# Sliding-window attention and an MLP-mixer on one core: side work planned into two thirds of the MLP, stores of the last batches on GpSimd's queue, more transpositions by DMA, loads begun sooner

## The chip, the core and the metric

The kernel runs on one core of a Trainium2 chip. The core has TensorE (matmuls, into PSUM), VectorE and ScalarE (which empty PSUM and do the elementwise work), GpSimd (here it issues the DMAs that cast), SyncE (SP, here it issues transposing DMAs and stores) and 16 DMA engines that all queues share. The metric is the device time of one execution in microseconds; the median of three runs before the change is 296.96 us.

## The reference

Eight batches of 576 positions and 8 heads of 64. First causal attention over a window of 128 positions with an ALiBi bias per head; then an MLP-mixer on the result (512 channels): a token MLP across positions, a residual, a channel MLP (512 to 1536 to 512), a residual. Inputs and output are float32.

```python
scores = np.matmul(q, k.T) / 8 - slope[h] * |i - j|     # only 0 <= i - j < 128
x = softmax(scores) @ v                                 # then heads side by side: [8, 576, 512]
h = np.maximum(x.T @ w_tok1, 0) @ w_tok2                # 576 -> 256 -> 576
u = x + h.T
out = u + np.maximum(u @ w_ch1, 0) @ w_ch2              # 512 -> 1536 -> 512
```

## The kernel before, in words

Two batches form a pair: 9 blocks of 128 positions, four per batch and one (`TAIL`) that holds the last 64 positions of both. A window of 128 means that a block attends to itself and to the block before it.

For each block `load` brings q, k and v with GpSimd's DMAs, which cast to bf16. `transposes` turns q and k so that the head dimension lies on partitions: on TensorE (8 transpositions, L455, into a PSUM bank that VectorE or ScalarE copies out, L460) or, from the block with number `FROM_QK` = 12 on, by a transposing DMA on SP's queue (L447). `scores` does the score matmuls (L485) into two double banks, ScalarE's exponential (L494) and VectorE's multiplication by the mask table (L500), which holds bias and window. `values` multiplies by v, whose extra column of ones gives the sums (L525), and VectorE divides (L529, L533; ScalarE can, L542).

`token_mix` does the token MLP of a batch (L561 and L568, relu L574 or L575; L599 and L595) and adds x, giving u (L617; for batch 0 with an identity matmul, L602, and a copy, L614). Then u is turned: by TensorE (4 transpositions per block, L634, copies L640) for batches under `FROM_U` = 4, by SP's transposing DMA (L625) for the rest.

`side(b)` is attention and token mixing of batch b. `main(b)` is its channel MLP: 12 hidden tiles of four 512-column matmuls (L682), relu (L687 or L688), three extra tiles for the tail block in odd batches (L697), then for each block 12 matmuls of the second layer in four groups of three (L718), the sum with u (L725), and a store by SP (L734, L732).

Nothing of this order is written by hand. `Plan` records every operation with an engine, a cost in ns, a rank and its buffers, and `Plan.run` lays them out in time: at each step it takes, over all engines, the operation that can start first, and at equal times the one with the lower rank. Buffers are rings; PSUM has four single banks and two double ones (`s0`, `s1`), one for each set of heads. Ranks of `main(b)` and of `side(b + 1)` both run along the length of `main(b)`, the side's over `SPREAD` = 0.93 of it, so the two are interleaved. Loads go out in a fixed order (`LOADS` for the first pair and the weights, then block by block), at most 8 in flight and 10 blocks ahead. An operation with `other` may go to a second engine. `emit` writes the instructions in planned order, and puts matmuls on zeros (L767) into planned gaps of TensorE in the first 60 us. The waits between engines follow from the buffers.

At the start raw q and k of block 0 come as float32 by SP and ScalarE (L347) and VectorE casts them (L396); GpSimd makes the identity and the distance table with five operations (L348 to L353) before its first load, and ScalarE makes the masks from the distances (L357).

Of the kernel before, what the change touches and what calls it, by code (L numbers as in the profile page):

```python
# [10 lines left out]
ALU = mybir.AluOpType  # L11
# [5 lines left out]
SPREAD = 0.93  # L17


class Buf:  # L20
    def __init__(self, ring):
        self.ring, self.slot = ring, None
        self.writers, self.parts, self.users = [], {}, []

    def __call__(self):
        return self.ring.slots[self.slot]


class Ring:
    def __init__(self, slots):  # L30
        self.slots = slots
        self.owner = [None] * len(slots)
        self.log = [[] for _ in slots]

# [8 lines left out]
    def best(self):  # L43
        got = [(t, i) for t, i in ((self.free(i), i) for i in range(len(self.slots))) if t is not None]
        return min(got) if got else None
# [6 lines left out]
class Plan:  # L52
# [3 lines left out]
    def ring(self, name, slots):  # L56
        self.rings[name] = Ring(slots)

    def buf(self, name):
        return Buf(self.rings[name])  # L60
# [45 lines left out]
    def dma(self, emit, descs, packets, makes=(), rewrites=(), order=None):  # L106
        o = self.op("POOL", 550 + 0.33 * descs, emit, 0, makes=makes, rewrites=rewrites,
                    order=order or self.slot())
        o.packets = packets
        return o  # L110

    def run(self):
# [21 lines left out]
        free = {"PE": 1500.0, "ACT": 5600.0, "DVE": 1600.0, "POOL": 2300.0, "SP": 1300.0}  # L134
        server, lanes, sent = SERVER, [], 0
        self.gaps = []
        mode = 0
        todo = len(ops)
        while todo:
            best = None  # L140
            for e, c in cand.items():
                pick = None
                for o in c:
                    if e == "POOL" and o is not pool[sent]:
                        continue
                    t = max(ready[o], free[e])
                    if o.other:
                        mine, its = (o.cost, o.other[1]) if e == o.eng else (o.other[1], o.cost)
                        that = o.other[0] if e == o.eng else o.eng
                        if max(ready[o], free[that]) + its < t + mine - (0 if e == o.eng else 1):  # L150
                            continue
                    for b in o.bufs:
                        if b.slot is None:
                            got = b.ring.best()
                            if got is None:
                                t = None
                                break
                            t = max(t, got[0])
                    if t is None:
                        continue  # L160
                    if e == "POOL" and len(lanes) >= 8:
                        t = max(t, lanes[-8])
                    key = (t if t > free[e] + 1e-6 else free[e], o.rank, o.n)
                    if pick is None or key < pick[0]:
                        pick = (key, o)
                if pick and (best is None or pick[0][0] < best[0][0]):
                    best = pick + (e,)
# [8 lines left out]
            for b in o.bufs:  # L176
                if b.slot is None:
                    b.slot = b.ring.best()[1]
                    b.ring.owner[b.slot] = b
                    b.ring.log[b.slot].append(b)  # L180
            if e == "PE":
                slow = 2.0 if t < WARM else 1.0
                if t > free[e] + 1.0:
                    self.gaps.append((free[e], t))
                    t += 60.0
                elif o.mode != mode:
                    t += 95.0
                mode = o.mode
                o.t0 = t
                free[e] = t + o.cost * slow  # L190
                o.done = free[e] + 165.0
            elif e == "ACT":
                o.t0, free[e], o.done = t, t + o.cost - 115, t + o.cost
            elif e == "DVE":
                o.t0, free[e], o.done = t, t + max(o.cost - 80, 50), t + o.cost
            elif e == "SP":
                o.t0, free[e] = t, t + o.cost
                if o.bus:
                    start = t + 300
                    o.done = start + min(3.3 * o.bus, o.bus + max(server - start, 0)) + 650  # L200
                    server = max(server, start) + o.bus
                else:
                    o.done = t + 2500
            else:
                o.t0 = t
                free[e] = t + o.cost
                server = max(server, t + 1000) + o.packets * PACKET
                o.done = server + 1500
                lanes.append(o.done)
                sent += 1  # L210
# [11 lines left out]
    def emit(self, spin):  # L222
        banks = self.rings["bank"]
# [15 lines left out]
WARM = 9000.0  # L239
HOLD = 2  # L240
FROM_QK = 12
FROM_U = 4
AHEAD = 10
FILL = 60000.0
SERVER = 4700.0
# [8 lines left out]
def kernel(  # L254
# [43 lines left out]
    plan.ring("bank", [psum.tile([P, DM], F32, name=f"bank{i}") for i in range(4)])  # L298
    for e in range(2):
        plan.ring(f"s{e}", [psum.tile([P, 2 * DM], F32, name=f"wide{e}")])  # L300
# [5 lines left out]
    ring("v", AHEAD, [P, H, D + 1])  # L306
# [15 lines left out]
    ident = const.tile([P, P], BF16, name="ident")  # L322
    dist = const.tile([P, 2, P], F32, name="dist")
# [21 lines left out]
    dve_.memset(zero[:, :], 0.0)  # L345
    for raw, t, eng in ((raws[0], q, nc.sync), (raws[1], k, nc.scalar)):
        eng.dma_start(out=raw[:, :, :], in_=rows(t, 0, 0, P))  # L347
    make_identity(nc, ident)  # L348
    nc.gpsimd.iota(dist[:, :, :], pattern=[[-P, 2], [1, P]], base=P, channel_multiplier=-1,
                   allow_small_or_imprecise_dtypes=True)  # L350
    nc.gpsimd.affine_select(out=dist[:, 0, :], in_=dist[:, 0, :], compare_op=ALU.is_gt,
                            fill=1.0e9, base=0, pattern=[[-1, P]], channel_multiplier=1)
    nc.gpsimd.affine_select(out=dist[:, 1, :], in_=dist[:, 1, :], compare_op=ALU.is_ge,  # L353
                            fill=1.0e9, base=0, pattern=[[1, P]], channel_multiplier=-1)
    for e in range(2):
        for i, h in enumerate(HEADS[e]):
            act_.activation(out=masks[e][:, i, :, :], in_=dist[:, :, :], func=ACT.Exp,  # L357
                            scale=-float(slopes[h]))
    for t in plan.rings["v"].slots:
        dve_.memset(t[:, :, D : D + 1], 1.0)  # L360

# [80 lines left out]
    def transposes(pr, blk, rank):  # L442
# [7 lines left out]
        tp = plan.buf("bank")  # L450

        def go():
            for i, n in enumerate("qk"):
                for hp in range(NHP):
                    pe_.transpose(tp().bitcast(BF16)[:, (i * NHP + hp) * P : (i * NHP + hp + 1) * P],  # L455
                                  got()[:, i, 2 * hp : 2 * hp + 2, :].rearrange("p h d -> p (h d)"),
                                  ident[:, :])

        def copy(eng=dve_.tensor_copy):
            eng(out=t().rearrange("p a b -> p (a b)"), in_=tp().bitcast(BF16))  # L460

        plan.op("PE", 8 * 56, go, rank, makes=tp, uses=[got])
        plan.op("DVE", 690, copy, rank, makes=t, uses=[tp], other=("ACT", 1025, lambda: copy(act_.copy)))

    def scores(pr, blk, half, rank, behind=()):
# [3 lines left out]
        sp = [plan.buf(f"s{e}") for e in range(2)]  # L469
# [36 lines left out]
    def values(pr, blk, half, e, pb, rank):  # L506
# [4 lines left out]
        ot, rt = plan.buf("bank"), plan.buf("rt")  # L511
# [10 lines left out]
        def go():  # L522
            mms = [(a, z, kind, vb, i, h) for a, z, kind, vb in work for i, h in enumerate(HEADS[e])]
            for m, (a, z, kind, vb, i, h) in enumerate(mms):
                pe_.matmul(view()[a:z, i, :], lhsT=pb[e]()[:, i, kind, a:z], rhs=vb()[:, h, :],  # L525
# [21 lines left out]
    def token_mix(b, rank):  # L547
# [4 lines left out]
        xt = plan.buf("xt")  # L552
        r1 = plan.buf(f"r1{half}")
        t1 = [plan.buf("bank") for _ in range(NJ)]
        tk = half if (pr == 0) else None
        plan.op("DVE", 260, lambda: dve_.tensor_copy(out=xt()[far, :], in_=xb()[own, TAIL, :]), rank(0),
                makes=xt, reads=[(xb, (TAIL, tk))])
# [8 lines left out]
        def tails():  # L566
            for j, rs, rhs in ((0, own, xb()[own, TAIL, :]), (1, far, xt()[far, :])):
                pe_.matmul(t1[j]()[:, :], lhsT=W1[rs, NC, j * P : (j + 1) * P], rhs=rhs, start=False, stop=True)  # L568

        plan.op("PE", 225, tails, rank(216), adds=t1, reads=[(xb, (TAIL, tk))], uses=[xt], needs=lw1,  # L570
                mode=1)
# [11 lines left out]
        for blk in blocks:  # L583
            wide = b == 0
            if wide and blk < 2:
                hts.append(plan.buf(f"s{blk}"))
            ht = hts[blk % 2] if wide else plan.buf("bank")
# [32 lines left out]
        for blk in blocks:  # L620
# [9 lines left out]
            ut = plan.buf("bank")  # L630
# [40 lines left out]
    def main(b, rank):  # L671
# [4 lines left out]
        r2t = plan.buf("r2t") if half else None  # L676
        for t in range(NHT):
            ct = plan.buf("bank")
# [6 lines left out]
            rk = rank(864)  # L685
            plan.op("PE", 862, go, rk, makes=ct, reads=[(uT, x) for x in blocks if x != TAIL], needs=[lc1[t]])
# [3 lines left out]
            if half and t % 4 == 3:  # L690
                cx = plan.buf("bank")
# [15 lines left out]
        for blk in blocks:  # L707
# [3 lines left out]
            for cols in cuts:  # L711
                o2 = plan.buf("bank")
# [16 lines left out]
                def store(blk=blk, ob=ob, cols=cols):  # L729
                    if blk == TAIL:  # L730
                        for i in range(2):
                            nc.sync.dma_start(out=out[2 * pr + i, NC * P : S, :], in_=ob()[i * R : (i + 1) * R, :])  # L732
                    else:
                        nc.sync.dma_start(out=out[b, (blk % NC) * P : (blk % NC + 1) * P, cols], in_=ob()[:, cols])  # L734

                plan.op("SP", 550, store, rk, uses=[ob])
# [64 lines left out]
```

## Time and profile before

| | |
|---|---|
| runs | 296.24, 296.96, 297.02 us |
| the profiled execution | 296.92 us, span 295.1 us |
| granted TensorE clock | 1.000 |
| TensorE busy | 285.9 us, 2490 matmuls |
| VectorE, ScalarE, GpSimd busy | 159.8, 136.1, 110.1 us |
| hidden layer, L682 | 384 matmuls, 92.9 us |
| second layer, L718 | 396 matmuls of 512 columns, 96.4 us |
| transpositions on TensorE | qk (L455) 104, u (L634) 72 |
| fillers, L767 | 28 |
| transposing DMAs on SP | 24 of qk, 18 of u |
| DMA | 36.67 MB, engines full until about 195 us |

A row of the lines' view gives line, engine, operation, tiles and shapes, the number, then busy us and mean ns of one. A matmul's duration there is longer than the interval from one to the next, since matmuls overlap; intervals are read from the chain of waits, which lists pieces in order of time. "US to landing" is the time from a DMA's issue to its completion.

### The profile page before, as it was taken

Reading aid. Unit: us, or ns where it says so; the run is one execution under the profiler, and the core shown is the slowest. Engines: PE = TensorE matmul, PEld = TensorE weight load, DVE = VectorE, ACT = ScalarE, POOL = GpSimd, SP = SyncE. Lnnn points to the kernel's source line nnn. Section 1 sums busy time; section 2 is a strip of 40 time slices with the busy share of each in tenths; the row PEclk is TensorE's granted clock in tenths of the full one; section 3 lists DMA queues with packets and bytes.
Section 4 is the critical chain, followed back from the end, with each engine's and each line's share of the span. In section 5 each row is a group of like instructions: output and inputs, shape, how many; then the busy total and the mean of one; then the engine's idle time right before and its main releaser. Section 6 shows DMA issues by size and latency. Waiting matters only on the chain.

```text
span 295.1 us, 6147 instructions
## 1 busy us (share of the span) xinstructions
PE 285.9 (97%) x2490; PEld 150.2 (51%) x2490; DVE 159.8 (54%) x364; ACT 136.1 (46%) x236; POOL 110.1 (37%) x140
## 2 busy tenths in 40 slices
PE   7999999999999999999999999999999999999995
PEld 2665454446664555455664445445664445435543
DVE  4697656735674466455773548254873556250022
ACT  5483884218940197008840087107850087105600
POOL 8998495976656257510585008000000000000000
PEclk9999999999999999999999999999999999999999
DMA  9999999999999999999999959955001510042013
GB/s 121 142 148 179 176 161 181 157 189 185 157 137 140 216 169 150 127 195 169 126 117 162 223 106 106 130 109 126 2 2 71 142 38 2 36 122 76 0 71 107
DMA packets 158011, 36.67 MB, mean 124 GB/s; under 512 B 148768, under 2 KB 153504, under 8 KB 157984
## 3 DMA queue, kind: packets, MB, share of 16 engines
q0 software_dynamic: 115376, 17.67, 87.9%
q1 hardware_dynamic: 41568, 18.36, 33.0%
q8 instruction: 19, 0.31, 0.4%
q10 hardware_dynamic: 1040, 0.26, 0.4%
q14 instruction: 8, 0.07, 0.1%
HBM read 35.85 MB, written 9.44 MB: 153 GB/s over the span
## 4 chain that ended last, share of the span: by engine, by line
PE 89%; DVE 5%; ACT 2%; DMA 2%; issue 1%
PE bank L718 31%; PE bank L682 28%; PE wide L485 6%; PE bank L525 5%; PE bank L599 4%; PE bank L561 4%; PE bank L697 4%; PE bank L455 2%; DVE pe L500 2%; DMA raw<-in_q_dram 1%; PE bank L634 1%; ACT pe L494 1%; PE bank L767 1%; PE bank L568 1%; DMA uT<-ub 1%; ACT xb L542 1%
## 5 line engine op out<-in xcount | busy, mean ns | idle before, releaser
L718 PE MATMUL bank<-WC,r 128*128 128x512 bf16 (+1 forms) x396 | 96.4, 373 | 0.0
L682 PE MATMUL bank<-uT,WC 128*128 128x512 bf16 x384 | 92.9, 379 | 2.4 <-DVE xb L533 1.0
L494 ACT ACTIVATE pe<-wide 128x1024 bf16<-128x1024 f32 (+1 forms) x74 | 63.3, 911 | 35.5 <-PE wide L485 35.4
L687 ACT ACTIVATE r<-bank 128x512 bf16<-128x512 f32 x75 | 44.5, 600 | 39.2 <-PE bank L682 36.4
L718 PEld LDWEIGHTS <-r 128*128 128x128 bf16 x396 | 37.2, 98 | 42.2 <-issue 3.1
L725 DVE TENSOR_TENSOR ob<-bank,ub 128x512 f32<-128x512 f32 (+1 forms) x37 | 25.1, 677 | 59.6 <-PE bank L718 59.3
L682 PEld LDWEIGHTS <-WC 128*128 128x128 bf16 x384 | 34.1, 98 | 37.5 <-issue 3.6
L381 POOL DMA_DIRECT2D v<-in_v_dram x40 | 34.5, 867 | 47.9 <-PE bank L525 36.2
L500 DVE TENSOR_TENSOR pe<-pe,mask 128x1024 bf16<-128x1024 bf16 (+1 forms) x66 | 39.3, 612 | 6.8 <-ACT pe L494 6.3
L381 POOL DMA_DIRECT2D qk<-in_q_dram x39 | 33.8, 867 | 15.4 <-DMA qk<-in_k_dram 9.5
L381 POOL DMA_DIRECT2D qk<-in_k_dram x39 | 33.4, 859 | 8.8 <-DMA v<-in_v_dram 3.4
L617 DVE TENSOR_TENSOR ub<-bank,xb 128x512 bf16<-128x512 f32 x32 | 21.7, 688 | 13.4 <-PE bank L599 11.9
L525 PEld LDWEIGHTS <-pe 128*128 128x128 bf16 (+1 forms) x552 | 22.9, 100 | 11.9 <-DVE pe L500 2.3
L525 PE MATMUL bank<-v,pe 128*128 128x65 bf16 (+1 forms) x552 | 26.9, 196 | 0.7 <-DVE xb L533 0.3
L533 DVE TENSOR_TENSOR xb<-bank,rt 128x256 bf16<-128x256 f32 (+1 forms) x62 | 25.6, 422 | 1.3
L688 DVE TENSOR_SCALAR r<-bank 128x512 bf16<-128x512 f32 x21 | 14.5, 688 | 17.6 <-PE bank L682 15.0
L574 ACT ACTIVATE r<-bank 128x512 bf16<-128x512 f32 x8 | 4.8, 597 | 38.8 <-PE bank L568 38.8
L561 PE MATMUL bank<-xb,W 128*128 128x512 bf16 x64 | 21.4, 380 | 0.1
L485 PEld LDWEIGHTS <-qkT 64*128 64x128 bf16 x552 | 15.1, 96 | 12.4 <-issue 8.0
L485 PE MATMUL wide<-qkT 64*128 64x128 bf16 (+1 forms) x296 | 19.8, 222 | 0.7 <-DVE qkT L460 0.7
L529 DVE RECIPROCAL rt<-bank 128x4 f32<-128x4 f32 (+1 forms) x74 | 11.7, 173 | 9.8 <-PE bank L525 9.5
L599 PE MATMUL bank<-r,W 128*128 128x512 bf16 x56 | 16.2, 379 | 0.0
(55 smaller groups left out, 193.6 us busy)
## 6 DMA issues: line engine op xcount, KB each, us to landing
out_dram<-ob SPq DMA_DIRECT2D x31, 256.0 KB, 3.1
v<-in_v_dram POOLq DMA_DIRECT2D x32, 128.0 KB, 7.9
qk<-in_q_dram POOLq DMA_DIRECT2D x31, 128.0 KB, 9.5
qk<-in_k_dram POOLq DMA_DIRECT2D x31, 128.0 KB, 9.4
WC<-in_moe_w_ch_dram POOLq DMA_DIRECT2D x8, 384.0 KB, 8.6
out_dram<-ob SPq DMA_DIRECT2D x10, 128.0 KB, 2.3
qk<-in_q_dram POOLq DMA_DIRECT2D x8, 64.0 KB, 7.3
qk<-in_k_dram POOLq DMA_DIRECT2D x8, 64.0 KB, 7.8
```

Source lines behind the costliest of these rows:

```text
L381: nc.gpsimd.dma_start(out=to()[p0 : p0 + n, :, :], in_=rows(src, b, s0, n))
L485: pe_.matmul(wide(e)[:, i, kind, a:z], lhsT=ts[kb]()[e * D : (e + 1) * D, NHP + i, :], rhs=ts[blk]()[e * D : (e + 1) * D, i, a:z], start=T ...
L494: act_.activation(out=pb[e]()[:, :, lo:, c0:c1_], in_=wide(e)[:, :, lo:, c0:c1_], func=ACT.Exp, scale=scale)
L500: dve_.tensor_tensor(out=o, in0=o, in1=mk[:, :, lo:, c0:c1_], op=ALU.mult)
L525: pe_.matmul(view()[a:z, i, :], lhsT=pb[e]()[:, i, kind, a:z], rhs=vb()[:, h, :], start=m == 0, stop=m == len(mms) - 1, skip_group_check=True)
L533: dve_.tensor_tensor(out=x4[r0:r1_, :, e, :], in0=view()[r0:r1_, :, 0:D], in1=rt()[r0:r1_, :, :].broadcast_to([r1_ - r0, 4, D]), op=ALU.mult)
L561: pe_.matmul(t1[j]()[:, :], lhsT=W1[:, c, j * P : (j + 1) * P], rhs=xb()[:, blk, :], start=c == 0, stop=False)
L599: pe_.matmul(ht()[:, hs], lhsT=W2[:, j, c * P : (c + 1) * P], rhs=r1()[:, j, :], start=j == 0, stop=j == NJ - 1 and not fold)
L682: pe_.matmul(ct()[:, :], lhsT=WC1[:, cb, t * P : (t + 1) * P], rhs=uT()[:, cb, :], start=cb == 0, stop=cb == NCB - 1)
L687: plan.op("ACT", 600, lambda t=t, ct=ct: act_.activation(out=r2()[:, t, :], in_=ct()[:, :], func=ACT.Relu), rk, part=(r2, t), uses=[ct], o ...
L718: pe_.matmul(o2()[:, cols], lhsT=l, rhs=WC2[:, t, cols], start=t == 0, stop=t == NHT - 1)
L725: plan.op("DVE", 160 + 530 * n / DM, lambda blk=blk, o2=o2, ob=ob, cols=cols: dve_.tensor_tensor(out=ob()[:, cols], in0=o2()[:, cols], in1 ...
```

## The change

Ten things are changed together:

- `SPREAD` goes from 0.93 to 0.65: ranks of the next batch's side work run over the first two thirds of the main part.
- `FROM_QK` 12 to 9, `FROM_U` 4 to 2: all qk blocks of the second pair, and u of batches 2 and 3, are turned by SP's DMAs.
- From batch `FROM_P` = 5 on stores go out on GpSimd's queue, behind all loads, except the last two blocks of the last batch.
- GpSimd does only one iota before its loads; VectorE makes distances and identity.
- Block 0 of the first pair is turned in two halves, q and then k, each copied by itself.
- The first three hidden tiles of batch 0 are done in quarter-width pieces, block by block as u is turned.
- Batch 0's token mixing no longer copies the tail rows to the other half; its two tail matmuls run one after the other.
- The planner lets an operation of batch 0's side work go ahead of one that could start sooner (`FIRST`, `GRACE`).
- PSUM is one tile of 8 banks; scores take either of two pairs; v is stored with rows of 128 elements per head instead of 65.
- Planner constants (starting times, SP's cost beside a transposition, `SERVER`).

```diff
-SPREAD = 0.93
+SPREAD = 0.65
...
-        free = {"PE": 1500.0, "ACT": 5600.0, "DVE": 1600.0, "POOL": 2300.0, "SP": 1300.0}
+        free = {"PE": 1500.0, "ACT": 5600.0, "DVE": 3300.0, "POOL": 1250.0, "SP": 1300.0}
...
+                    if o.rank < FIRST and (early is None or key < early[0]):
+                        early = (key, o)
+                if early and early[1] is not pick[1] and early[0][0] < pick[0][0] + GRACE * pick[1].cost:
+                    pick = early
...
-                o.t0, free[e] = t, t + o.cost
+                o.t0 = t
+                free[e] = t + (1310.0 if o.bus or t < turned + 150 else o.cost)
                 if o.bus:
+                    turned = free[e]
...
+FIRST = -5e5
+GRACE = 0.6
+PIECES = 3
 HOLD = 2
-FROM_QK = 12
-FROM_U = 4
+FROM_QK = 9
+FROM_U = 2
+FROM_P = 5
...
-SERVER = 4700.0
+SERVER = 4200.0
...
-    plan.ring("bank", [psum.tile([P, DM], F32, name=f"bank{i}") for i in range(4)])
-    for e in range(2):
-        plan.ring(f"s{e}", [psum.tile([P, 2 * DM], F32, name=f"wide{e}")])
+    ps = psum.tile([P, 8, DM], F32, name="ps")
+    plan.ring("ps", [ps[:, i, :] for i in range(8)],
+              lambda s: ps[:, s[0] : s[1] + 1, :].rearrange("p a b -> p (a b)"))
+    ONE, TWO = [(4,), (5,), (6,), (7,)], [(0, 1), (2, 3)]
...
-    ring("v", AHEAD, [P, H, D + 1])
+    ring("v", AHEAD, [P, H, 2 * D])
...
-    make_identity(nc, ident)
-    nc.gpsimd.iota(dist[:, :, :], pattern=[[-P, 2], [1, P]], base=P, channel_multiplier=-1, ...)
-    nc.gpsimd.affine_select(out=dist[:, 0, :], ...)
-    nc.gpsimd.affine_select(out=dist[:, 1, :], ...)
+    nc.gpsimd.iota(diff[:, :], pattern=[[1, P]], base=0, channel_multiplier=-1, ...)
+    dve_.tensor_scalar(out=cut[:, 1, :], in0=diff[:, :], scalar1=0.0, scalar2=1.0e9, op0=ALU.is_lt, op1=ALU.mult)
+    dve_.tensor_scalar(out=cut[:, 0, :], in0=diff[:, :], scalar1=0.0, scalar2=1.0e9, op0=ALU.is_ge, op1=ALU.mult)
+    dve_.tensor_tensor(out=dist[:, 1, :], in0=diff[:, :], in1=cut[:, 1, :], op=ALU.max)
+    dve_.scalar_tensor_tensor(out=dist[:, 0, :], in0=diff[:, :], scalar=float(P), in1=cut[:, 0, :],
+                              op0=ALU.add, op1=ALU.max)
+    dve_.tensor_scalar(out=ident[:, :], in0=diff[:, :], scalar1=0.0, scalar2=None, op0=ALU.is_equal)
...
+        halves = [(0,), (1,)] if pr == 0 and blk == 0 else [(0, 1)]
+        for at, which in enumerate(halves):
...
+            plan.op("PE", 4 * n * 56, go, rank, makes=tp, part=(got, "turned"), **src)
+            plan.op("DVE", 110 + 290 * n, copy, rank, uses=[tp], **more,
+                    other=("ACT", 172 + 427 * n, lambda copy=copy: copy(act_.copy)))
...
+        first = []
+        if b == 0:
+            first = [bank() for _ in range(PIECES)]
+            for blk in blocks:
+                for t, ct in enumerate(first):
+                    def go(t=t, ct=ct, blk=blk):
+                        for cb in range(NCB):
+                            pe_.matmul(ct()[:, blk * P : (blk + 1) * P], lhsT=WC1[:, cb, t * P : (t + 1) * P],
+                                       rhs=uT()[:, cb, blk * P : (blk + 1) * P],
+                                       start=cb == 0, stop=cb == NCB - 1)
...
+                late = b >= FROM_P and blk not in blocks[-2:] or FROM_P <= b < B - 1
+                q_ = nc.gpsimd if late else nc.sync
...
-                plan.op("SP", 550, store, rk, uses=[ob])
+                if late:
+                    plan.dma(store, P, 1024, uses=ob)
+                else:
+                    plan.op("SP", 550, store, rk, uses=[ob])
```

## The prediction, made before the changed kernel had been run

> **What bounds the kernel now.** I read the page first (busy times, slices, the chain's shares), then the busy time by stretch, then the chain of waits in order of time, then the DMA issues. The page (parts 1, 2 and 4):
>
> ```profile
> PE 285.9 (97%) x2490; PEld 150.2 (51%) x2490; DVE 159.8 (54%) x364; ACT 136.1 (46%) x236; POOL 110.1 (37%) x140
> PE   7999999999999999999999999999999999999995
> DMA  9999999999999999999999959955001510042013
> PE 89%; DVE 5%; ACT 2%; DMA 2%; issue 1%
> ```
>
> TensorE is the bound in every slice; VectorE and ScalarE have room on the mean. The DMA row matters too: the engines are full until about 200 us and nearly empty behind. So TensorE work taken off is worth its time, but work given to DMA before 200 us meets a full resource. Busy time by stretch (length, then PE, PEld, DVE, ACT, POOL; clock; DMA share; GB/s):
>
> ```profile
> 64.00:169.00 105.00, 105.00 (x983) 56.14 (x981) 62.74 (x137) 48.73 (x74) 51.13 (x61) 1.00 1.84 161
> 169.00:200.00 31.00, 29.78 (x234) 14.25 (x230) 16.95 (x37) 13.94 (x26) 6.14 (x7) 1.00 0.95 116
> 200.00:270.00 70.00, 68.78 (x572) 35.35 (x573) 36.16 (x78) 32.31 (x60) 0.00 (x0) 1.00 0.23 64
> ```
>
> From 64 to 169 us TensorE never stops; from 169 to 270 it idles 2.4 us. The chain in order of time (start, us, what) says where, and gives the price of one matmul by line:
>
> ```profile
> 27.69 0.67 PE bank L634 x12
> 28.36 0.45 PE bank L455 x8
> ...
> 51.84 1.40 PE bank L718 x6
> ...
> 58.96 5.18 PE bank L718 x24
> ...
> 169.68 0.68 DVE xb L533 x2
> 170.43 3.61 PE bank L682 x16
> ...
> 197.39 2.83 DMA uT<-ub
> 200.35 3.61 PE bank L682 x16
> ```
>
> A 128-column transposition costs 0.67/12 = 56 ns on TensorE (L634; L455 the same), a 512-column matmul 5.18/24 = 216 ns. L682 is the first matmul of a batch's hidden layer: at 200.35 it starts when the last transposition of u lands (200.22). Last, the DMA issues: all of them, then single ones by a window on their issue (at 40.3, 59.1, 162.2 and 167.3 us):
>
> ```profile
> qkT<-qk SPq DMA_TRANSPOSE x24, 8.4
> uT<-ub SPq DMA_TRANSPOSE x16, 2.5
> ```
> ```profile
> WC<-in_moe_w_ch_dram POOLq DMA_DIRECT2D x1, 384.0 KB, 9.4
> ```
> ```profile
> qkT<-qk SPq DMA_TRANSPOSE x1, 8.5
> ```
> ```profile
> uT<-ub SPq DMA_TRANSPOSE x1, 5.4
> ```
> ```profile
> uT<-ub SPq DMA_TRANSPOSE x1, 3.0
> ```
>
> A transposition of qk takes 3.0 us on empty engines (the one issued at 200.7) and 8.5 beside loads. All uT here were issued after 162 us, as the loads ran out: 5.4 us for the first, 3.0 for the fourth.
>
> **Part by part.** The sum stands against the profiled execution's own time, 296.92 us (span 295.1 and 1.82 around it); the median of the runs is 296.96, the same.
>
> *TensorE work off.* Three qk blocks (8 transpositions each) and the nine u blocks of batches 2 and 3 (4 each) leave TensorE: 60 x 56 ns = 3.36. The hidden layer of batch 0 does three tiles as 48 quarter-width matmuls (48 x 57) in place of 12 x 216: +0.14. All of it lay in stretches where TensorE never idles: **-3.2**. The DVE and ACT copies that go with them (L460 0.69 x3, L640 0.42 to 0.59 x9) were hidden by TensorE and cost nothing either way.
>
> *The start.* GpSimd issues its first load at 2.29, behind five operations of 0.2 to 0.35 us; only a smaller iota stays, so about 1.1: loads begin up to 1.2 sooner. VectorE gets five 128x128 operations (0.25 each by its rows of that size, 1.3 in all) and is idle 1.9 us there before its first cast: no cost; above 1.9 each further us would delay the chain by one. Loads follow each other at 0.87 us, so the shift is kept. How far can TensorE follow? The fourth weight piece of the second layer lands at 40.32+9.4 = 49.7; the matmuls that need it start at 51.84. Moved to 48.5 it allows at most 51.84-48.5 = 3.3. For the other end: the first loads now share the engines with the two raw transfers (landing 4.53 and 4.97, before any load's packets), which can delay the first cast by some 0.5, with nothing won: +0.5. Within that, splitting the first turning into q and k lets copies and transpositions overlap (one 0.70 copy becomes two, half beside the transposition: about 0.7), batch 0's hidden layer starts as blocks come, and the built order has 24 fillers (L767) instead of 28, of which 10.6 us passed before. One loss: batch 0's two half-row matmuls (0.32 as a pair at 23.81) now run one after the other, +0.1, for a copy of 0.26 saved. The wider v rows, the one PSUM tile with the same two pairs and four single banks, and the planner's preference for batch 0's side work change no instruction's size: nothing of their own. I take **-2.5**, near the load's end, since TensorE stood 2.1 us behind its load there.
>
> *Boundaries of batches 4 to 7.* At 169.35, 199.5, 236.2 and 265.1 TensorE waits 1.1, 0.8, 0.5 and 0.3 for transposed u: 2.7. In the new order 36 second-layer matmuls (7.8 us) stand between the last token-mixing matmul and the next hidden layer, and in batches 5 and 6 no store stands between the transpositions on SP (0.53 to 0.6 each). Four transpositions 1.3 apart with 2.4 to 3.0 landing need 7: covered. **-2.4** (0 to -2.7).
>
> *The moved stores.* Fourteen stores of batches 5 to 7 go behind the last load on GpSimd's queue, which is issued by 192 us, well before the first of them. No 256 KB store from GpSimd is in the trace; its 128 KB loads on emptier engines land in 3.4 (issued 141.8 and 177.2), its 256 KB ones in 5.1 beside others. The output ring has three buffers at 2.6 us per block (12 x 216 ns) = 7.8; add 0.69 and 5.1 and it still fits: 0 (to +1). The last two blocks stay on SP, so the end is as before. The Trainium skill (DMA: Bandwidth & Descriptors, Issuing engine by pattern) speaks against this: a simple store belongs on Sync, GpSimd's first byte coming at about 1 us against 0.6; by it fourteen stores land 0.4 later each (an estimate), and the sum is unchanged, since none is waited for.
>
> *New waits.* (a) Batch 2's u is now turned by four transfers in the full stretch. The built order leaves 36 second-layer matmuls and 24 half-height score matmuls, 7.8+0.9 = 8.7 us, between its last token-mixing matmul and its hidden layer. The first transposition can be issued some 0.1 after that matmul (add 0.69, first of four), the last 3.9 later (1.3 each on SP): 4.0. Landing: 2.4 at best (no wait); 8.5 each and 4.1 apart, as two qk transpositions issued 3.2 apart landed (83.4 and 87.5), gives 0.1+8.5+12.3-8.7 = 12.2 of wait. uT moves half of qkT's bytes and its one half-loaded row is 5.4: I take 7, so 4.0+7-8.7 = **+2.2**. Queued behind it is all of TensorE. (b) Batch 3 has 12.8 us from its first token-mixing pair to the hidden layer, and the last transposition is issued at 5.9 (first sum ready 1.4, three steps of 1.3, a store of 0.6 between): 5.9+7-12.8, about zero; **+0.4** (0 to 10). (c) Loads give way to three more qk transpositions: from 59.0 to 83.6 fifteen 128 KB loads landed, 24.6 us against 13 at 0.87; less some 2.5 for four stores, five transpositions cost 1.8 each. So pair 1's tail block shifts by 3 x 1.8-1.2 = +4.2; its transposition landed at 76.3, now 80.5, and the new order, counted at the rows' intervals, uses it 18.2 us of matmuls after batch 1's main part begins (64.1-2.5+18.2 = 79.8): **+0.8** (0 to 4). (d) The side work stands in a shorter stretch: in an odd batch's hidden layer ScalarE gets nearly 19 us (17 activations of 0.60, ten of 0.91, less what VectorE takes) beside 20 of TensorE by the built order, 17 beside 19 before. Where it was as dense (240 to 250, 8.5 of 10 busy) one wait of 0.3 appeared. Six such phases: **+0.8** (0 to 4).
>
> The Trainium skill (same page, Queues, rings and completion order) says that each DMA engine takes turns between queues packet by packet. That alone would about double a transposition's 2.4 to 4.8 (an estimate), (a) would be 0.1 and the sum lower by 2.1; the rows show 3.0 becoming 8.5, and I go by the rows.
>
> Sum: -3.2-2.5-2.4+2.2+0.4+0.8+0.8 = -3.9; 296.92-3.9 = **293.0**. A measurement of this kernel can't tell changes under 0.3% (0.9 us) from none.
>
> **Rivals.** *Quick transfers:* uT lands as in the rows behind 162 us (3 to 5.4), (a) to (c) vanish: -3.2-2.5-2.4+0.8 = -7.3, 289.6 (287.5 to 291). For it: the 1:2 size. Against: full engines until 200. *Dense side work:* the gain of order is eaten by TensorE waiting for ScalarE and VectorE, (d) at its end of 4: 296.2 (295 to 298). For it: ScalarE at 93% of the phase. Against: 105 us without one idle moment at 90%. *Slower:* u of batches 2 and 3 queues behind the loads. With qkT's spacing of 4.1, (a) is 12.2 and (b) some 9: 296.92-8.1+12.2+9+1.6 = 311; it decides once (a) to (d) together pass 8.1, that is at a spacing of about 2.6 rather than 1.3. Against: u is half the size. *No earlier start:* raw transfers delayed as much as loads gain: +3 on the forecast, 296.0.
>
> **How the numbers follow.** Forecast (291 to 295, its own range) 0.45; quick transfers 0.22; dense side work or no earlier start (295 to 298) 0.15; slower 0.18. The range 288.3 to 298.5 leaves out some 0.04 below and 0.16 above. Faster by over 0.3% (under 296.0): 0.45+0.22+0.06 = 0.73; same 0.08; slower 0.19.
>
> **What would show it.** L482 with 80 and L670 with 36 matmuls at 56 ns; first load near 1.1; the second layer of batch 0 by 49.3; no TensorE wait at the starts of batches 4 to 7; uT issued near 90 us landing in about 7 with a wait of 2 before L731. Wrong would make it: uT landings over 9 us there, a late raw q (first cast after 5.0), or ScalarE ending many TensorE waits in the hidden phases.

## The result and the profile after

The changed kernel takes 299.94 us (median of four runs, 299.61 to 300.30) against 296.60 of the kernel before in the same runs: a ratio of 1.0113 (95% interval 1.009 to 1.0135). It is slower, by 1.1%. The profiled execution has 300.30 us and a span of 298.5. The page, parts 1, 2 and 4:

```profile
PE 284.2 (95%) x2462; PEld 149.3 (50%) x2462; DVE 151.3 (51%) x350; ACT 137.6 (46%) x246; POOL 116.7 (39%) x150
PE   6989999999999789998999999999999999999995
PEclk9999999999999979999999999999999999999999
DMA  9999999999999999999999689969002320451013
PE 79%; ACT 9%; DVE 5%; DMA 4%; issue 2%; SPq 1%; ACTq 0%
```

TensorE has less to do (28 matmuls fewer in count, and cheaper ones) and yet ends later: ScalarE now has 9% of the chain where it had 2%, and slice 15 of the clock row, from 104 to 112 us, is a 7. Busy time by stretch (length, PE, PEld, DVE, ACT, POOL; clock; DMA share; GB/s):

```profile
64.00:97.00 33.00, 32.75 (x321) 17.82 (x320) 17.92 (x41) 17.69 (x29) 18.36 (x21) 1.00 1.82 165
97.00:130.00 33.00, 30.32 (x233) 14.53 (x232) 17.40 (x39) 14.17 (x23) 17.58 (x22) 0.95 1.95 171
130.00:169.00 39.00, 37.20 (x335) 19.78 (x334) 19.28 (x41) 16.91 (x33) 15.14 (x19) 1.00 1.68 171
169.00:200.00 31.00, 31.00 (x240) 14.69 (x238) 15.97 (x35) 13.50 (x21) 6.15 (x7) 1.00 0.93 134
200.00:270.00 70.00, 69.16 (x584) 35.08 (x583) 36.30 (x78) 31.25 (x53) 4.96 (x9) 1.00 0.32 68
```

Before, TensorE was busy without a break from 64 to 169 us and idle for 2.4 us from 169 to 270; now it is nearly the other way round: 4.7 us of idle time lie between 64 and 169, where in one stretch the clock is 0.95, and 0.8 from 169 to 270. TensorE's own waits (us in total, times, longest):

```profile
PE ps L519 <- ACT pe L528: 2.9, 6, 0.7
PE ps L731 <- DMA uT<-ub: 1.7, 1, 1.7
PE ps L731 <- DVE ob L775: 1.3, 1, 1.3
```

None of the first kind was there before: no score matmul waited for an exponential. The third row is one to read with care. It stands at the start of batch 3's hidden layer, 137.45 us, where VectorE had been done for 0.57 us; the last transposition of u was issued at 129.50 and took 7.9, so that it landed at 137.36. It is the DMA again.

To see where the time comes from I take each batch's start of the hidden and of the second layer, less the matmuls issued before it at their intervals (216, 56 or 29 ns, and 96+120 for a change to 64-row score matmuls and back). What is left is time in which TensorE did nothing useful ("grown by" is what the gap to the kernel before gained since the row above, in us):

| up to | before: at | without work | after: at | without work | grown by, against before |
|---|---|---|---|---|---|
| hidden layer 0 | 29.70 | 15.9 | 28.39 | 15.0 | -0.9 |
| second layer 0 | 48.08 | 16.8 | 48.90 | 17.4 | +1.5 |
| hidden layer 1 | 63.98 | 17.8 | 65.23 | 19.0 | +0.5 |
| second layer 1 | 83.23 | 17.9 | 84.93 | 19.1 | 0 |
| hidden layer 2 | 101.92 | 18.2 | 105.45 | 22.9 | +3.5 |
| second layer 2 | 117.70 | 18.2 | 123.66 | 24.7 | +1.8 |
| hidden layer 3 | 132.42 | 18.1 | 137.45 | 26.2 | +1.5 |
| second layer 3 | 151.55 | 18.3 | 158.70 | 27.2 | +0.9 |
| hidden layer 4 | 170.43 | 19.4 | 173.39 | 27.2 | -1.1 |
| second layer 5 | 218.38 | 20.4 | 224.82 | 28.5 | +0.4 |
| last matmul | 291.59 | 21.7 | 294.80 | 28.3 | -1.5 |

Idle time grows by 6.6 us, work shrinks by 3.4, and the tail is 0.15 longer: the span's +3.4.

The chain of waits in order of time, around the start of batch 0's hidden and second layers and of batch 2's hidden layer:

```profile
32.98 1.59 ACT r L737 x3
34.56 0.81 ACT xb L576 x4
35.42 2.75 PE ps L731 x12
...
53.10 1.40 PE ps L768 x6
...
97.59 7.73 DMA uT<-ub
105.45 3.14 PE ps L731 x8
```

The transpositions, by the DMA view: those of batch 2 (issued 93.4 to 97.7), of batch 3 (118 to 135), and all after 190 us with the stores from GpSimd (us to landing at the end):

```profile
uT<-ub SPq DMA_TRANSPOSE x4, 7.6
```
```profile
uT<-ub SPq DMA_TRANSPOSE x4, 7.0
```
```profile
out_dram<-ob POOLq DMA_DIRECT2D x7, 256.0 KB, 2.3
uT<-ub SPq DMA_TRANSPOSE x12, 2.4
```

7.6 and 7.0 with the engines full, 2.4 with them empty. And TensorE's timeline ahead of batch 2's hidden layer (in brackets the idle time just before and what ended it), with the clock in three windows there (the column before the last two):

```profile
101.55 0.40 PE L519 MATMUL ps<-qkT 64*128 64x128 bf16 x8
102.63 0.21 PE L519 MATMUL ps<-qkT 64*128 64x128 bf16 x1 [0.68 <-ACT pe L528]
103.12 0.21 PE L519 MATMUL ps<-qkT 64*128 64x128 bf16 x1 [0.28 <-ACT pe L528]
105.45 3.14 PE L731 MATMUL ps<-uT,WC 128*128 128x512 bf16 x8 [1.73 <-DMA uT<-ub]
```
```profile
104.00:105.00 1.00, 0.00 (x0) 0.00 (x0) 0.00 (x0) 1.00 (x2) 0.00 (x0) 1.00 2.07 153
106.00:107.00 1.00, 1.00 (x4) 0.29 (x2) 0.08 (x1) 0.00 (x0) 0.00 (x0) 0.50 1.34 297
110.00:111.00 1.00, 1.00 (x22) 0.66 (x19) 0.83 (x3) 0.89 (x2) 0.59 (x1) 1.00 1.60 158
```

Between 101.75 and 105.45 TensorE had some 0.5 us of matmuls. Behind it the eight hidden matmuls take 3.14 us instead of 1.73: the clock is 0.50 until 109.3.

### The profile page after: what moved, and what is told of

The parts are those of the page before. It is cut to its first block, busy times and chain, and to the rows that moved or that the text cites. A ratio compares the mean times of both kernels' runs of the same rounds, so it can differ in the third digit from the quotient of the medians.

```text
span 298.5 us, 6114 instructions
## 1 busy us (share of the span) xinstructions
PE 284.2 (95%) x2462; PEld 149.3 (50%) x2462; DVE 151.3 (51%) x350; ACT 137.6 (46%) x246; POOL 116.7 (39%) x150
## 4 chain that ended last, share of the span: by engine, by line
PE 79%; ACT 9%; DVE 5%; DMA 4%; issue 2%; SPq 1%; ACTq 0%
PE ps L768 29%; PE ps L731 25%; PE ps L519 5%; PE ps L596 4%; ACT pe L528 4%; PE ps L635 4%; PE ps L559 4%; DMA uT<-ub 3%; PE ps L747 2%; ACT xb L576 2%; ACT r L737 2%; PE ps L482 1%; DMA raw<-in_q_dram 1%; DVE pe L534 1%; DVE ob L775 1%
## 5 line engine op out<-in xcount | busy, mean ns | idle before, releaser
L737 ACT ACTIVATE r<-ps 128x512 bf16<-128x512 f32 x85 | 50.8, 615 | 102.6 <-PE ps L731 98.3
L731 PE MATMUL ps<-uT,WC 128*128 128x512 bf16 x372 | 92.8, 384 | 3.5 <-DMA uT<-ub 1.7
L768 PE MATMUL ps<-WC,r 128*128 128x512 bf16 (+1 forms) x396 | 89.2, 373 | 0.2 <-DVE ob L775 0.2
L528 ACT ACTIVATE pe<-ps 128x1024 bf16<-128x1024 f32 (+1 forms) x74 | 63.8, 927 | 18.1 <-PE ps L519 18.0
L775 DVE TENSOR_TENSOR ob<-ps,ub 128x512 f32<-128x512 f32 (+1 forms) x37 | 25.0, 677 | 64.1 <-PE ps L768 64.0
L559 PE MATMUL ps<-v,pe 128*128 128x65 bf16 (+1 forms) x552 | 27.1, 196 | 0.8 <-ACT xb L576 0.5
L653 DVE TENSOR_TENSOR ub<-ps,xb 128x512 bf16<-128x512 f32 x34 | 22.8, 687 | 9.9 <-PE ps L635 9.8
L567 DVE TENSOR_TENSOR xb<-ps,rt 128x256 bf16<-128x256 f32 (+1 forms) x61 | 25.0, 420 | 1.1
L519 PE MATMUL ps<-qkT 64*128 64x128 bf16 (+1 forms) x296 | 20.8, 221 | 3.5 <-ACT pe L528 2.9
L596 PE MATMUL ps<-xb,W 128*128 128x512 bf16 x64 | 19.2, 379 | 0.4 <-ACT xb L576 0.4
L635 PE MATMUL ps<-r,W 128*128 128x512 bf16 x64 | 17.9, 379 | 0.0
```

The source lines that it names most:

```text
L519: pe_.matmul(wide(e)[:, i, kind, a:z], lhsT=ts[kb]()[e * D : (e + 1) * D, NHP + i, :], rhs=ts[blk]()[e * D : (e + 1) * D, i, a:z], start=T ...
L528: act_.activation(out=pb[e]()[:, :, lo:, c0:c1_], in_=wide(e)[:, :, lo:, c0:c1_], func=ACT.Exp, scale=scale)
L567: dve_.tensor_tensor(out=x4[r0:r1_, :, e, :], in0=view()[r0:r1_, :, 0:D], in1=rt()[r0:r1_, :, :].broadcast_to([r1_ - r0, 4, D]), op=ALU.mult)
L596: pe_.matmul(t1[j]()[:, :], lhsT=W1[:, c, j * P : (j + 1) * P], rhs=xb()[:, blk, :], start=c == 0, stop=False)
L635: pe_.matmul(ht()[:, hs], lhsT=W2[:, j, c * P : (c + 1) * P], rhs=r1()[:, j, :], start=j == 0, stop=j == NJ - 1 and not fold)
L731: pe_.matmul(ct()[:, :], lhsT=WC1[:, cb, t * P : (t + 1) * P], rhs=uT()[:, cb, :], start=cb == 0, stop=cb == NCB - 1)
```

## Experiments

Theory A: the transpositions of u of batches 2 and 3, landing late among the loads, are the main loss. Rival B: the side work squeezed into 0.65 of the main part loses by itself. Rival C: the new start loses.

### u of batches 2 and 3 on TensorE again

```diff
-FROM_U = 2
+FROM_U = 4
```

> The changed kernel with FROM_U back at 4: u of batches 2 and 3 is turned on TensorE again, all else as changed. Theory A (the transfers of u in the stretch of full DMA engines are what the change loses: 3.5 us of wait ahead of batch 2, 1.8 of half clock behind it, 2.2 around batch 3): TensorE gets 36 transpositions x 56 ns = 2.0 back, the waits and the half clock go, about 300 - 7.5 + 2.0 = 294.5, granted clock 1.0 throughout. Rival B (the squeezed side work, SPREAD 0.65, is what loses, and the transfers only lie in its wake): TensorE still waits at the boundaries of batches 2 and 3, now for VectorE and ScalarE, and the time stays at 299 to 302. Rival C (the new start is what loses): no change there, about 299.5.

Measured: 296.09 us (eight runs), 0.9977 of before (0.9959 to 0.9995), clock 1.000. Batch 2's hidden layer starts at 102.17, batch 3's at 132.67: 3.3 and 4.8 us sooner than in the changed kernel, although 36 transpositions are back. A holds, 1.6 us short in size: score matmuls still wait for ScalarE,

```profile
PE ps L519 <- ACT pe L528: 1.9, 4, 0.6
```

and this is a second loss, which none of the three theories named. B and C as written fall: neither allowed for a gain of 3.8 us from these transpositions alone.

### The loads made small

```diff
-                nc.gpsimd.dma_start(out=to()[p0 : p0 + n, :, :], in_=rows(src, b, s0, n))
+                m = 16 if pr >= 2 else n
+                nc.gpsimd.dma_start(out=to()[p0 : p0 + m, :, :], in_=rows(src, b, s0, m))
```

> The changed kernel with the loads of pairs 2 and 3 (issued from about 80 us on) cut to 16 of their 128 rows; number, order and plan as before, the other rows keep old data, so batches 4 to 7 are computed from leftovers. If the transpositions of u land late because loads fill the DMA engines: uT of batches 2 and 3 lands in 2.4 to 3.5 us instead of 7 to 7.7, the waits ahead of batches 2 and 3 and the half clock go, 293.5 to 296. If the late landing belongs to SP's queue itself (the qk transpositions and stores ahead in it): it stays at 6 or more and the time at 299 to 300.5.

Measured: 294.65 us, 0.9941 (0.9923 to 0.9958), clock 1.000. The same transpositions of batches 2 and 3, in the same order on SP (issued in 85 to 110 and 118 to 135):

```profile
uT<-ub SPq DMA_TRANSPOSE x4, 3.7
```
```profile
uT<-ub SPq DMA_TRANSPOSE x4, 2.3
```

Batch 2's hidden layer starts at 103.67 and batch 3's at 132.53, with no TensorE wait for u. So it is the loads in the engines that make the landing late, not what stands ahead on SP's queue: of the changed kernel's time up to 5.3 us hang on it, waits and clock together. (Small loads could also free other things; but 4.9 of the 5.3 are won by the start of batch 3's hidden layer, and from there to the last matmul the two profiles take the same time.)

### Fillers in the wait

```diff
             def go(t=t, ct=ct):
+                for _ in range(8 if b == 2 and t == 0 else 0):
+                    pe_.matmul(ct()[:, :], lhsT=zero[:, 0:P], rhs=zero[:, :], start=True, stop=True)
```

> The changed kernel with 8 matmuls on zeros (1.7 us) put ahead of batch 2's first hidden tile, inside the wait for its u; order and plan otherwise the same. If the half clock from 105.9 to 109.3 us follows from TensorE's idling before it, the clock stays at 1.0 there and 1.7 us go: 298.2. If it has another cause, or if the fillers only move the wait, the time stays within 0.5 of 299.9.

Measured: 298.17 us (seven runs). Batch 2's hidden layer still starts late (fillers from 103, its last u lands as before, and the first tile follows), but the clock stays up:

```profile
106.00:108.00 2.00, 2.00 (x17) 1.05 (x15) 1.80 (x3) 0.60 (x1) 0.68 (x1) 1.00 1.49 195
```

Batch 2's second layer starts at 121.67 instead of 123.66. The half clock was a consequence of the idle stretch, and cost 1.8 of the 3.3 us by which the changed kernel is slower than the one before.

### SPREAD back

```diff
-SPREAD = 0.65
+SPREAD = 0.93
```

> The changed kernel with SPREAD back at 0.93, u of batches 2 and 3 still by transfer. Theory A (late transfers in full engines): worse, since side work ends later and the same 7 to 8 us landing finds less second-layer work to hide in: waits of 5 us or more at batches 2 and 3, 303 to 308. Rival B (the squeeze is the loss): better than 300, 296 to 298.

Measured: 316.54 us. A's direction, but eight beyond its range: hidden layers 2, 3 and 4 start at 109.5, 145.2 and 188.3, the clock falls three times (mean 0.962), and score matmuls wait for ScalarE far more often:

```profile
PE ps L519 <- ACT pe L528: 13.9, 22, 0.8
```

So the early side work is what makes the late transpositions bearable at all, and the new waits of the scores do not come from squeezing: they are worse without it.

### SPREAD 0.65 alone

```diff
 # the kernel before
-SPREAD = 0.93
+SPREAD = 0.65
```

> The kernel before with SPREAD 0.65 alone, all transpositions and stores as before. If the boundary term holds by itself (waits of 1.1, 0.8, 0.5 and 0.3 us ahead of batches 4 to 7 go because u is ready sooner): 294.0 to 294.8. If the squeeze costs as much in the hidden phases, by waits for ScalarE and VectorE: 296 to 297.5.

Measured: 293.65 us, 0.9911 (0.9889 to 0.9933). That is 0.35 under the range of its first theory. B falls for good: this one constant gives 2.7 us. The hidden layers of batches 4 to 7 start at 168.51, 197.89, 233.53 and 262.92; the time without work grows from batch 3's hidden layer to the end by about 0.4 us (18.5 to 18.9), where it grew by 3.6 before.

### Either pair of banks, or a fixed one

Where do the scores' waits come from? `scores` asks for two double banks. Before, each set of heads had its own ring of one. In the changed kernel both ask one ring, "either of two pairs", and `Plan.run` looks up the earliest free pair for each of them before either is taken. It finds the same pair twice, so the second pair's later time doesn't count, and the group is planned once one pair is free. On the chip TensorE then issues the first score matmul and stands in order at the second until ScalarE has emptied the other pair. TensorE's timeline of the changed kernel shows it, here at the start:

```profile
15.88 0.23 PE L519 MATMUL ps<-qkT 64*128 64x128 bf16 x1
16.56 0.21 PE L519 MATMUL ps<-qkT 64*128 64x128 bf16 x1 [0.46 <-ACT pe L528]
```

Of the six waits (2.9 us) two lie at the start (1.1, at 16.56 and 19.35), two just ahead of batch 2's hidden layer (1.0, in the timeline above) and two in the hidden layers of batches 3 and 5 (0.8, at 148.16 and 211.35).

```diff
-        sp = [bank(TWO) for _ in range(2)]
+        sp = [bank([TWO[e]]) for e in range(2)]
```

> The changed kernel with one line changed: the two sets of heads take a fixed double bank each, as before the change, in place of either. Theory: with either pair allowed the planner looks up the earliest free pair for both sets, finds the same one twice, and so lets a score group start when one pair is free; on TensorE's in-order queue the second score matmul then waits for ScalarE (2.9 us in six waits in the changed kernel, none before). Fixed pairs take these six waits away: 297 to 298.5. Rival (ScalarE is late anyway, and the wait only moves to the matmul behind): 299.4 to 300.5.

> As e9, with u of batches 2 and 3 on TensorE too (FROM_U 4). If the two losses are separate they add: e1's 296.1 less 1.5 to 2.5 gives 293.5 to 294.6, and no score matmul waits for ScalarE. If the pairs don't matter: 295.8 to 296.4.

Measured, with u still by transfer: 298.80 us (ten runs, 296.33 to 300.88), 1.0064 (1.0033 to 1.0096), 0.3 above its range. The profile is that of the fastest of the ten, and why they lie so far apart is open. In it no score matmul waits for ScalarE any more, but the wait for batch 2's u is now 3.2 in one piece: the score waits there had covered a part of it. With u on TensorE: 293.55 us (ten runs), 0.9913 (0.9888 to 0.9939). TensorE's longest kinds of wait there, the second being the filler's at the start:

```profile
PE ps L559 <- DVE pe L534: 1.3, 4, 0.5
PE ps L823 <- DVE zero L375: 1.2, 1, 1.2
```

The theory holds: 0.5% and 0.6% of the time (1.5 and 1.9 us) for one line, and the two losses add, 1.0113 to 0.9913. The first of the two steps is within the noise at its edge (1.009 to 1.0135 against 1.0033 to 1.0096); the second, 0.9977 to 0.9913, is clear of it.

### The start

```diff
 # e6: the kernel before, with one iota on GpSimd, tables on VectorE, and
-        free = {"PE": 1500.0, "ACT": 5600.0, "DVE": 1600.0, "POOL": 2300.0, "SP": 1300.0}
+        free = {"PE": 1500.0, "ACT": 5600.0, "DVE": 3300.0, "POOL": 1250.0, "SP": 1300.0}
-SERVER = 4700.0
+SERVER = 4200.0
 # e7: the changed kernel with FROM_U = 4 and
-GRACE = 0.6
+GRACE = -1e9
 # e2: the changed kernel with
-PIECES = 3
+PIECES = 0
```

> The kernel before with the new start alone (one iota, tables on VectorE, the planner's starting times and SERVER of the changed kernel; no halves, no pieces, no GRACE). Loads land 0.3 to 1.6 us sooner, as in the changed kernel. Theory of the prediction (TensorE follows the loads): batch 1's main part begins 1 to 2.5 us sooner, 294.5 to 296. Rival (the start is bound by the chain through ScalarE and VectorE, not by loads): within 0.5 of the kernel before, or slower by a new order, 296 to 298.

> As e1 (u of batches 2 and 3 on TensorE) with GRACE at -1e9, so that no operation of batch 0's side work goes ahead of one that could start sooner. If the preference makes TensorE, VectorE and ScalarE wait for operations that come later than planned (TensorE waits of 0.67 and 0.83 us near 15.9 and 18.5 us): batch 1's main part begins 0.5 to 1.5 us sooner than e1's 64.5 and the time is 294.5 to 295.5. If the preference helps: 296.5 to 298.

> The changed kernel with PIECES = 0: batch 0's first three hidden tiles as whole tiles again. Theory: the pieces begin 1.3 us sooner but end together, so that three activations in a row and three held banks stop TensorE near 33 to 35.4 us; without them batch 0's second layer begins 1 to 2 us sooner (47 to 48 instead of 48.9) and the whole takes 298 to 299. Rival: the wait there comes from late score and value work on ScalarE (the copies with four activations), not from the pieces: the second layer begins at 48.9 or later, 300 to 301.

Measured: e6 296.88, 1.0025 (1.0012 to 1.0038), the rival's case: earlier loads alone win nothing. In its profile batch 1's hidden layer starts at 63.50, 0.5 sooner than before, and TensorE's longest kind of wait is for VectorE's multiplication of the scores, where it was 0.2 before:

```profile
PE bank L528 <- DVE pe L503: 2.5, 4, 1.0
```

e7 295.87, 0.9982 (0.9966 to 0.9998), against e1's 0.9977: the preference does nothing, a miss of both expectations. Every engine's instructions come in the same order in the two traces, so these are two measurements of one order.

e2 302.27, above both expectations: the second layer of batch 0 begins 0.75 us sooner (48.15), short of the 1 to 2 expected, and batch 1 0.7 sooner, but its waits ahead of batches 2 and 3 are 2.9 and 2.5 instead of 1.7 and 1.3 and the half clock lasts twice as long, so that its total says nothing of the pieces. What they are worth with fixed pairs and u on TensorE was not tried.

The new start does win something, once the score waits are out of it. With fixed pairs (e9, e10) batch 1's hidden layer starts at 62.95 and 62.80; in the kernel before it is 63.98, and 64.10 in e5's profile, which has the same order up to there. With either pair it is 65.23 in the changed kernel and 63.83 in e8. So the new start is worth about 1.2 us at this point; which part of it does that was not tried.

### The three qk blocks, and the best version

```diff
 # e8: the changed kernel with FROM_U = 4 and
-FROM_QK = 9
+FROM_QK = 12
 # e11: the kernel before with SPREAD = 0.65 and
-FROM_QK = 12
+FROM_QK = 9
```

> As e1 with FROM_QK back at 12 as well: three qk blocks of pair 1 on TensorE again. If those three transfers are won for nothing (their DMA time is hidden, 24 x 56 ns = 1.3 us of TensorE saved): 1.3 slower than e1, about 297.4. If they hold the loads and pair 1's last blocks up: as e1 or faster, 294.5 to 296.

> The kernel before with two constants changed: SPREAD 0.65 and FROM_QK 9. If the three qk transfers are won as between e8 and e1 (298.3 against 296.1), with 1.3 from TensorE's matmuls alone: e5's 293.65 less 1.3 to 2.2, 291.4 to 292.4. If pair 1's last blocks then land too late for side work that is planned sooner: 293.5 to 295.

Measured: e8 298.30, 1.0069 (1.0045 to 1.0092); e11 293.08, 0.9906 (0.9871 to 0.9941). Turning pair 1's three qk blocks by transfer gains 2.2 us between e8 and e1, and only 0.6, within the intervals and short of the 1.3 to 2.2 expected, between e5 and e11 (by the ratios 0.9911 and 0.9906, hardly anything); that it doesn't lose more than the noise is shown, its size is not. e11, two constants of the kernel before, e10, and e5, one constant, are the best versions, 3.5, 3.0 and 2.7 us under their runs of the kernel before (0.9906, 0.9913, 0.9911), and each beats both kernels; the runs do not tell the three apart. So all the gain of the ten changes that these runs can tell from noise comes from `SPREAD`; the new start, the moved stores and the qk blocks together add nothing to it that is clear of noise.

## Why the prediction was wrong

It forecast 293.0, in 288.3 to 298.5, faster with 0.73; the kernel takes 299.9. The steps that failed are the start (3.6 us off in the profile, the largest miss), the clock behind batch 2's wait (1.8, in no term), the sizes of the waits for u of batches 2 and 3 (1.1 each), and the price of nothing for the new PSUM rings. By its own steps:

- **TensorE work, -3.2:** right. 80 and 36 transpositions remain, the count at the rows' intervals gives -3.4.
- **The start, -2.5:** wrong, in this profile it was about +1.1. But for the very first (0.4 later), loads that land before 57 us came 0.1 to 1.9 us sooner, and the fourth second-layer piece landed at 47.95 (1.7 sooner), but its matmuls began at 53.10, 1.3 later: TensorE stood 5.1 us behind its load instead of 2.1. The step read that 2.1 as room to close up; it was a sign that TensorE was waiting for something else. What the runs show in its place: the chain above has ScalarE, with three activations and four copies in a row between 32.98 and 35.42 while the banks of the pieces are held; 1.1 us are the score waits at 16.56 and 19.35, from the planner's look-up; and up to 1.4 us may be this profile's own start (last section). e6, which has the sooner loads and the tables on VectorE but no halves, pieces or preference, wins nothing. Without the score waits the new start is worth about -1.2 by batch 1's hidden layer, half of what was taken.
- **Boundaries of batches 4 to 7, -2.4:** right, e5 has it alone with 2.7.
- **The moved stores, 0:** consistent. They land in 2.2 to 2.7 us, SP's in the same trace behind 195 us in 1.7 to 3.5 (some are half the size), and no wait of TensorE goes back to them; they were not tried alone.
- **(a) batch 2's u, +2.2:** right in mechanism and landing (7 taken, 7.6 measured), one under in size. TensorE was free at about 102.1 and got u at 105.45: 3.3. The last transposition was issued 3.9 after the end of the last token-mixing matmul, as reckoned (4.0), but took 7.7, and TensorE had 8.4 of work from there, not 8.7.
- **What (a) brings with it, not in the sum:** the half clock, +1.8. The prediction asked of each wait who is queued behind, but not what idling does to the clock. The Trainium skill (TensorE: Matmul & The Clock Gate, Part 1: The HAM clock gate) says that the array falls to half rate after about 3.4 us without enough work, and returns after as long a busy time; here it fell behind 3.7 nearly idle us and stayed down for 3.4, which agrees. It was in reach: the kernel itself fills gaps of TensorE in its first 60 us with matmuls on zeros.
- **(b) batch 3's u, +0.4:** 1.5, with a landing of 7.9 for 7.
- **(c) pair 1's tail, +0.8:** not seen; TensorE's waits for qk transpositions are 0.4 us.
- **(d) dense side work, +0.8:** wrong in cause. The table grows by 1.3 up to the second layers of batches 3 and 5 (0.9 and 0.4), and 0.8 of it are score waits, from the planner's look-up of the double banks, not from ScalarE's share: e5 and e10 have the same `SPREAD` and no such wait. The failing step is the sentence that the one PSUM tile with "the same two pairs" costs "nothing of [its] own". No instruction changed its size, but the planned start of the score groups did; by e9 and e10 that costs 1.5 to 1.9 us in all, and most of the waits lie in the start and ahead of batch 2.

The rival that was slower had the right sign by the wrong price: batch 2's transpositions landed 1.3 to 1.5 us apart, as forecast, not 4.1.

## What to carry to other kernels

A full transfer resource can't be given work that something waits for soon: a transposition that lands in 2.4 us on empty engines took 7.6 among loads, and two microseconds of matmuls saved on the bound engine cost close to six. When a load lands two microseconds ahead of its use, ask first what TensorE waits for there: here sooner loads alone won nothing. In a planned kernel a change of buffers is a change of the plan: look for what the planner believes of when they are free.

## What the runs showed of the hardware that was not expected

One wait can cost twice: 3.3 us of wait brought 3.4 us at clock 0.50 behind it, and eight useless matmuls in the wait gave 1.8 us back (e4).

The start is not the same from run to run. Up to batch 1 e8 issues the changed kernel's instructions in the same order, yet its first transposition starts at 4.90 us and its next block's at 10.36, in 0.61 us (full clock); in the changed kernel's profile they are at 5.45 and 12.07, the latter in 1.06 us (half clock). TensorE's timeline of e8, then of the changed kernel:

```profile
4.90 1.10 PE L482 MATMUL ps<-ident,qk 128*128 128x128 bf16 x8 [0.53 <-DVE qk L421]
10.36 0.61 PE L482 MATMUL ps<-ident,qk 128*128 128x128 bf16 x8
```
```profile
5.45 1.04 PE L482 MATMUL ps<-ident,qk 128*128 128x128 bf16 x8 [1.09 <-DVE qk L421]
12.07 1.06 PE L482 MATMUL ps<-ident,qk 128*128 128x128 bf16 x8
```

Batch 1's hidden layer starts at 63.83 in the one and 65.23 in the other, and at 64.51 in e1, again in the same order; the first full-clock entry in the trace's record of the granted clock begins at 5.28, 13.77 and 8.97 us in the three. So about 1.4 us of any comparison of two single profiles may be this, which is why the start's +1.1 above is no more than "no gain", and why e6's ten runs, not its profile, decide what the loads are worth. That the clock alone is the reason is not shown: the kernel before and e5, in one order too, have it at 13.71 and 4.79 and start that layer at 63.98 and 64.10. What sets the moment of the clock's rise was not tried.
